# Block-sparse attention with a feed-forward layer: instruction order pinned on every engine, and values gathered from an on-chip copy in place of indirect DMA

## The chip, the cores and the metric

The kernel runs on one core of a Trainium2 chip. Times are device microseconds (us). A kernel's time is the median of its runs; a profile is one execution, with its own span. TensorE does the matrix products, VectorE (DVE) and ScalarE (ACT) the element-wise work, GpSimd (POOL) the gathers, and SyncE (SP) issues transfers. PEclk is the clock that TensorE was granted, as a share of full speed.

## The reference

```python
# q, k, v: [4, 8, 768, 64] float32; blocks of 32, so 24 blocks; 3 random blocks for each query block
mask = |block_i - block_j| <= 1, or block_i or block_j in {0, 23}, or block_j in sampled_blocks[block_i]
attn = softmax(where(mask, q @ k.T / 8, -1e9)) @ v          # per batch and head
x    = attn.transpose(0, 2, 1, 3).reshape(3072, 512)
out  = gelu_exact(x @ w_in[512, 2048]) @ w_out[2048, 512]
```

## The kernel before

A batch is worked in two halves of 384 query rows. For each half, the attention of the next half is merged with the output product of this one, and the hidden layer (x times w_in, 64 matmuls) is merged with "fill" steps: transposes of q and k for the next batch, and gathers. A scheduler decides the final order on each engine from the traced order and its own estimates.

Values are gathered from DRAM, one indirect DMA for each of the 11 query blocks of a half, and keys by two calls on GpSimd for each head pair:

```python
    def gather_v(b, hb, st):
        vg = vg_pool.tile([P, NQH, VROW], BF16, tag="vg", name="vg")
        for i in range(NQH):                       # 11 indirect DMAs
            nc.gpsimd.indirect_dma_start(out=vg[:, i, :], in_=v_dram[b][:, :], in_offset=...idx_v[:, qi:qi + 1]...)

    def gather_k(b, hb, hp, st):
        dv = kg.rearrange("p n (s c) -> p (n s) c", c=BLOCK)
        kv = kt.rearrange("p (n c) -> p n c", c=BLOCK)
        nc.gpsimd.indirect_copy(dv[:, 0:32, :], kv, idx_k[:, hb, 0:2], ...)    # 32 indices of 32 bf16
        nc.gpsimd.indirect_copy(dv[:, 32:44, :], kv, idx_k[:, hb, 2:3], ...)   # 12 indices
```

One q or k tile of a head pair is transposed: VectorE permutes it (`pm`), TensorE transposes six squares into PSUM (`ps`), and VectorE copies the result out (`tk` or `tq`); for k it also copies the two global blocks (`kgl`).

```python
    def transpose_qk(b, hp, which, tile_in, st):
        nc.vector.tensor_copy(pm, tile_in[:, 2 * hp:2 * hp + 2, :].rearrange(...))
        for j in range(NT):
            nc.tensor.transpose(ps[:, j, :], pm[:, j, :, :]..., ident)
        nc.vector.tensor_copy(dst.rearrange(...), ps.rearrange(...))
        if which == "k":
            ...                                    # kgl: two small copies out of dst
# ... cut ...
        merge(hidden_steps(b, hb, st), fill)
        if half + 1 < 2 * B:
            merge(attention_steps(nb_, nhb, sts[nb_]), output_steps(b, hb, st))
```

The softmax here doesn't subtract the row's maximum and nothing guards it: scores larger than these inputs give would overflow.

## Time and profile before

| | before |
|---|---|
| time, median of 3 | 408.56 us (406.87 to 408.6) |
| span of the profiled execution, mean clock | 429.1 us, 0.877 |
| TensorE busy / GpSimd busy | 67% / 48% |
| first hidden layer starts (profile) | 64.3 us |

From the page of the profiled execution: busy time by engine, and the span in 40 slices, where a digit is the busy tenths of a slice (PEclk: tenths of full clock).

```profile
span 429.1 us, 8099 instructions
...
PE 288.6 (67%) x3532; PEld 174.0 (41%) x3568; DVE 148.2 (35%) x327; ACT 142.9 (33%) x192; POOL 206.7 (48%) x212
...
PE   0273279324737376910949967699679999899996
...
POOL 8457675671577745665454373556722055500000
PEclk9999999655686779775899996969979999999999
```

TensorE is full only in the last quarter. The stretches from one hidden layer to the next, by engine (busy us, number of instructions, granted clock, DMA share and GB/s), say how much longer the early stages are than the last undisturbed one, 29.6 us:

```profile
64.00:137.40 73.40, 39.95 (x395) 23.20 (x397) 17.48 (x38) 16.53 (x22) 43.20 (x40) 0.67 0.76 158
137.40:212.90 75.50, 40.14 (x491) 23.63 (x496) 20.91 (x42) 19.34 (x26) 44.15 (x39) 0.75 0.48 107
...
374.70:404.30 29.60, 28.31 (x368) 16.76 (x372) 8.16 (x18) 16.32 (x22) 0.61 (x1) 1.00 0.08 28
```

What engines waited for (total us, times, longest) names two causes: gathered rows that come by indirect DMA, and a VectorE that stands at a value copy until its load has landed, with TensorE behind it for 20.1 us.

```profile
DVE v_pj L235 <- DMA st_v<-in_v_dram: 37.4, 3, 23.0
...
PE og L354 <- DMA vg<-v_dram_186,idx_v: 20.2, 17, 4.7
PE od L376 <- DVE xd L344: 20.1, 1, 20.1
...
PE ps L268 <- DVE pm L264: 7.5, 3, 4.0
```

### The profile page before, as it was taken

The page shows a single profiled execution, that of the slowest core. Times are in us where ns is not written, and L with a number is a line of the kernel's source. Part 1 is how long each engine was busy: PE and PEld are TensorE (multiplying, and loading weights), DVE is VectorE, ACT ScalarE, POOL GpSimd, SP SyncE. Part 2 cuts the span into 40 slices and gives each one's busy share as a digit, 9 for nine tenths or more (in the row PEclk, how much of TensorE's full clock was granted, in tenths as well). Part 3 has the DMA queues.
Part 4 walks back from the last instruction along what each step waited for, and adds up shares of the span by engine and source line. Part 5 has one row for each costly group of instructions (what it writes and reads, how often), then busy time and mean ns, then how long its engine had stood idle before and what let it go on. Part 6 is the DMA issues. An engine that isn't in the chain of part 4 may idle for free. (4 is left out here: it accounts for less than half of the span.)

```text
span 429.1 us, 8099 instructions
## 1 busy us (share of the span) xinstructions
PE 288.6 (67%) x3532; PEld 174.0 (41%) x3568; DVE 148.2 (35%) x327; ACT 142.9 (33%) x192; POOL 206.7 (48%) x212
## 2 busy tenths in 40 slices
PE   0273279324737376910949967699679999899996
PEld 0251165202423143500526534355345556555552
DVE  2693140102713054201514514447224436603301
ACT  1041125502200045510027503643247167267240
POOL 8457675671577745665454373556722055500000
PEclk9999999655686779775899996969979999999999
DMA  8935289139598764225433370501400100000101
GB/s 124 193 82 114 71 134 202 34 104 177 128 187 256 212 80 83 76 62 86 150 112 42 77 226 26 73 26 52 124 14 27 49 2 28 26 26 26 50 2 74
DMA packets 30805, 39.04 MB, mean 91 GB/s; under 512 B 4657, under 2 KB 24369, under 8 KB 30769
## 3 DMA queue, kind: packets, MB, share of 16 engines
q0 software_dynamic: 20960, 25.35, 31.5%
q1 hardware_dynamic: 9616, 13.02, 8.9%
q8 instruction: 28, 0.46, 0.4%
q10 hardware_dynamic: 192, 0.13, 0.1%
q14 instruction: 9, 0.07, 0.0%
HBM read 42.51 MB, written 9.62 MB: 121 GB/s over the span
## 5 line engine op out<-in xcount | busy, mean ns | idle before, releaser
L439 PE MATMUL hp<-xT,w_in_sb 128*128 128x384 bf16 x512 | 94.4, 341 | 27.9 <-ACT g L441 17.5
L286 POOL INDIRECT_COPY kg<-tk,idx_k 128x1024 bf16 x32 | 56.4, 1763 | 112.5 <-issue 44.0
L441 ACT ACTIVATE g<-hp 128x768 bf16<-128x768 f32 x64 | 51.5, 811 | 170.6 <-PE hp L439 76.3
L455 PE MATMUL op<-w_out_sb,g 128*128 128x512 bf16 x348 | 93.2, 396 | 6.0 <-issue 4.2
L439 PEld LDWEIGHTS <-w_in_sb 128*128 128x128 bf16 x512 | 51.5, 102 | 65.5 <-issue 36.0
L455 PEld LDWEIGHTS <-g 128*128 128x128 bf16 x384 | 34.3, 101 | 33.5 <-issue 6.4
L354 PEld LDWEIGHTS <-pt 128*32 128x32 bf16 (+1 forms) x992 | 28.7, 103 | 37.8 <-issue 24.3
L287 POOL INDIRECT_COPY kg<-tk,idx_k 128x384 bf16 x32 | 36.9, 1154 | 14.6 <-issue 13.3
L306 DVE TENSOR_TENSOR pt<-pt,mask_x 128x768 bf16<-128x768 bf16 x32 | 22.9, 723 | 61.0 <-ACT pt L305 58.6
L268 PE MATMUL ps<-ident,pm 128*128 128x128 bf16 x192 | 19.0, 256 | 24.6 <-DVE ident L110 15.9
L269 DVE COPY tk<-ps 128x768 bf16<-128x768 bf16 x16 | 15.3, 955 | 53.8 <-PE ps L268 23.0
L354 PE MATMUL og<-vg,pt 128*32 128x65 bf16 x704 | 18.9, 207 | 20.6 <-DMA vg<-v_dram_186,idx_v 20.2
L459 DVE COPY os<-op 128x512 f32<-128x512 f32 x24 | 16.6, 690 | 33.2 <-PE op L455 26.2
L256 POOL DMA_INDIRECT vg<-v_dram_189,idx_v x22 | 21.2, 963 | 12.9 <-PE og L354 6.7
L256 POOL DMA_INDIRECT vg<-v_dram_188,idx_v x22 | 21.4, 973 | 12.4 <-PE og L354 6.4
L268 PEld LDWEIGHTS <-pm 128*128 128x128 bf16 x192 | 15.3, 115 | 27.6 <-DVE pm L264 14.4
L256 POOL DMA_INDIRECT vg<-v_dram_187,idx_v x22 | 21.8, 989 | 7.4 <-issue 6.4
L376 PE MATMUL od<-v_nat,pd 128*64 128x65 bf16 x192 | 11.1, 215 | 20.1 <-DVE xd L344 20.1
L256 POOL DMA_INDIRECT vg<-v_dram_186,idx_v x22 | 21.3, 968 | 6.5 <-issue 6.5
L343 DVE RECIPROCAL rc<-og 128x6 f32<-128x6 f32 x32 | 6.1, 192 | 46.8 <-PE og L354 46.7
L316 PEld LDWEIGHTS <-kg 64*128 64x128 bf16 x704 | 12.7, 96 | 19.0 <-POOL kg L286 7.3
L376 PEld LDWEIGHTS <-pd 128*64 128x64 bf16 x192 | 9.1, 127 | 23.5 <-issue 22.6
(333 smaller groups left out, 347.4 us busy)
## 6 DMA issues: line engine op xcount, KB each, us to landing
out_dram<-os SPq DMA_DIRECT2D x24, 256.0 KB
st_v<-in_v_dram POOLq DMA_DIRECT2D x4, 768.0 KB
st_k<-in_k_dram POOLq DMA_DIRECT2D x3, 768.0 KB
st_q<-in_q_dram POOLq DMA_DIRECT2D x3, 768.0 KB
w_in_sb<-in_moe_w_in_dram POOLq DMA_DIRECT2D x4, 512.0 KB
w_out_sb<-in_moe_w_out_dram POOLq DMA_DIRECT2D x4, 512.0 KB
v_dram_186<-v_pj SPq DMA_DIRECT2D x1, 780.0 KB
v_nat<-v_dram_186 SPq DMA_DIRECT2D x1, 780.0 KB
```

The lines of the kernel that those rows point to most:

```text
L256: nc.gpsimd.indirect_dma_start(out=vg[:, i, :], out_offset=None, in_=v_dram[b][:, :], in_offset=bass.IndirectOffsetOnAxis(ap=idx_v[:, qi:q ...
L268: nc.tensor.transpose(ps[:, j, :], pm[:, j, :, :].rearrange("p h d -> p (h d)"), ident)
L269: nc.vector.tensor_copy(dst.rearrange("p (n j) -> p n j", j=NT), ps.rearrange("p j n -> p n j"))
L286: nc.gpsimd.indirect_copy(dv[:, 0:32, :], kv, idx_k[:, hb, 0:2], i_know_this_is_slow=True)
L287: nc.gpsimd.indirect_copy(dv[:, 32:44, :], kv, idx_k[:, hb, 2:3], i_know_this_is_slow=True)
L306: nc.vector.tensor_tensor(pt[:, 0, :, 0:HALF], pt[:, 0, :, 0:HALF], mask_x[:, hb * MH:hb * MH + MH, :].rearrange("p m c -> p (m c)") .unsq ...
L354: nc.tensor.matmul(o, lhsT=l, rhs=r, start=first, stop=True, skip_group_check=True)
L376: nc.tensor.matmul(od[:, 0, h, :], lhsT=pd[:, h, t, :], rhs=v_nat[:, t, 2 * hp + h, :], start=(t == 0 and h == 0), stop=True, skip_group_c ...
L439: nc.tensor.matmul(hp_[:, i, 0:HALF], lhsT=w_in_sb[:, ki, (m + i) * P:(m + i + 1) * P], rhs=xT[:, ki, :], start=(ki == 0), stop=(ki == KIN ...
L441: nc.scalar.activation(g[:, m:m + 2, :], hp_[:, :, 0:HALF], AF.Gelu)
L455: nc.tensor.matmul(op, lhsT=g[:, k, ti * P:ti * P + P], rhs=w_out_sb[:, k, :], start=(k == 0), stop=(k == KOUT - 1))
L459: nc.vector.tensor_copy(os, op)
```

## The change

The intent: (1) hold every engine to the traced order, so that nothing waits at a late load that the trace places later; (2) remove the 88 indirect DMAs: the values of a batch are written to DRAM once, spread onto the chip four times, rotated, over four groups of 32 partitions (16 transfers of 192 KB), and gathered from there by GpSimd in three calls for each half; (3) gather keys in one call with pairs of bf16 taken as f32; (4) refine the merging: more and smaller steps. The diff, cut to its core:

```diff
+class InOrder:
+    def __getattr__(self, name):
+        f = getattr(self._eng, name)
+        def call(*args, **kwargs):
+            return self._tc.keep_in_program_order(f(*args, **kwargs))
+        return call
...
+    pe, dve, act, pool, sp = (
+        InOrder(tc, e) for e in (nc.tensor, nc.vector, nc.scalar, nc.gpsimd, nc.sync))
...
+    def spread_v(b):
+        for c in range(4):
+            for s in range(4):
+                i = 6 * ((c - s) % 4)
+                sp.dma_start(out=v_rep[32 * s:32 * s + 32, i:i + 6, :],
+                             in_=v_dram[b][:, :].rearrange("(t c r) w -> c r t w", c=4, r=BLOCK)[c])
+    def natural_v(b, eng):                     # v_nat and vgl: copies of v_rep in natural order
...
     def gather_v(...):
-        for i in range(NQH):
-            nc.gpsimd.indirect_dma_start(...)
+        pool.indirect_copy(v_gat[hb].bitcast(F32)[...], v_rep.bitcast(F32)...,
+                           idx_v[:, hb, 2 * c:2 * c + 2], ...)      # c = 0, 1, 2
...
     def gather_k(...):
-        nc.gpsimd.indirect_copy(dv[:, 0:32, :], kv, idx_k[:, hb, 0:2], ...)
-        nc.gpsimd.indirect_copy(dv[:, 32:44, :], kv, idx_k[:, hb, 2:3], ...)
+        pool.indirect_copy(kg.bitcast(F32)..., st["k", hp].bitcast(F32)..., idx_k[:, hb, 0:3], ...)
...
+            if hb == 0:
+                fill += gv + gk                 # gathers of the next half, values first
+                if more:
+                    fill.append(prep_v(b + 1)); fill.append(spread_v(b + 1))
+                    if b > 0:
+                        fill += transpose_steps(b + 1)[:6]
+            elif b == 0:
+                for hp in range(NPAIR):
+                    fill += tr[2 * hp:2 * hp + 2] + [gk[hp]]
+                fill += gv + [lambda: natural_v(b + 1, dve)]
+            else:
+                fill += ([natural_v(b + 1, dve)] + transpose_steps(b + 1)[6:] if more else []) + gv + gk
```

In the start, in the changed kernel, ScalarE makes the first natural-order copies, and the first batch's eight q and k loads come as f32 by the SyncE and ScalarE queues.

## The prediction

> **What bounds it now.** TensorE, but only where it is fed. Busy times by 10 us stretch: from 340 to 420 us it is 92 to 100% busy at full clock; from 80 to 210 us about half, and the granted clock falls to 0.5 in stalls (mean 0.877). The undisturbed stage (second half of the last batch) takes 29.7 us from hidden layer to hidden layer in the chain of work that ended last. Eight stages of 30 to 34 us need about 250 us; the profile shows 364 us from the first hidden layer (64 us) to the end, so about 110 us are stalls. The timelines name them:
> - Pool: eleven indirect DMAs per half, 1.26 us apart (13.9 us), TensorE following row by row (38–47, 85–97 us); four key gathers, 5.19 us each start to start (20.8 us).
> - Order: VectorE stands at a value copy waiting for its load (37.4 us in the groups, longest 23.0); TensorE idles 20.1 us at 184–204 us.
>
> **What the change does.** It removes the 88 indirect DMAs (111 us of Pool) and adds 24 gathers from a fourfold on-chip copy, refilled by 3.1 MB of DMA per batch. Key gathers become one 44-index call in f32. From the trace, 32 indices take 3.65 us and 12 take 1.52 (start to start, 32 elements each): 0.107 us an index. The Trainium skill (GPSIMD Engine Reference, section Performance pitfalls for Q7 kernels) gives about 102 cycles per small read command, so I take it as mostly per index: estimated 4.5 us per key gather, 10 us per half for values. Pool then needs about 28 us per half plus 2.4 of load issues, against 35 before: still close to TensorE's 31. If the cost is per element, it is 21 us and Pool is off the path.
>
> Pinned order removes the waits at late loads, runs gathers a half ahead, and interleaves finer. One exponential less per head pair (0.27 us) is off the path. At the start, weighted sums still wait for value write, spread and three gathers: first hidden layer at about 55 us against 64.
>
> New costs: VectorE gets the natural-order copies, and its two-input and two-port operations collide with denser gathers (Trainium skill, SBUF — State Buffer, section Who interferes with whom). The trace agrees: the mask product took 2.54 us under a gather, 0.56 alone. Six of a batch's transposes sit in the last three hidden steps; at about 1.75 us of VectorE each (0.4 + 0.95 + 0.4) they hold the in-order TensorE some 6 us per batch.
>
> **Sum.** 55 start + 250 TensorE stages + 10 VectorE-bound transposes + 10 waiting for Pool (mostly values in batch 1) + 4 tail = 329 us in a profile. The profiled run of before was 5% above the timed ones; a kernel with fewer DMA waits should lose less, so I take 2%.
>
> Predicted **322 us, 8 in 10 between 300 and 348**. Faster by over 2%: 0.96; within 2%: 0.025; slower: 0.015.
>
> **What would show it.** Right: TensorE busy above 85% and mean clock near 0.97 after 60 us; key gathers about 4.5 us start to start; longest TensorE waits on gathered values in batch 1 and on VectorE at the ends of even hidden stages; no 20 us hole. Wrong: key gathers at 2.6 us with Pool idle half the time (then about 305); or Pool solid and TensorE waiting on gathered tiles in every half (then about 345).
>
> **What would make it wrong.** Gather cost per call; port collisions stretching VectorE and Pool; the refill of the copy landing late, so that value gathers slip a stage; loads queued behind waiting gathers on Pool.

## The result, and the profile after

| | before | after |
|---|---|---|
| median, same chip | 407.99 us (406.87 to 408.6) | 374.64 us (369.54 to 377.65) |
| ratio of the fast runs | | 0.909, 95% interval 0.902 to 0.916 |
| span of the profile, clock | 429.1 us, 0.877 | 375.9 us, 0.962 |
| TensorE / GpSimd busy | 67% / 48% | 76% / 29% |
| first hidden layer | 64.3 us | 71.7 us |

A ratio is the mean time of one kernel's fast runs over that of the other's in the same rounds, so it is not quite the ratio of the medians. The kernel became 9% faster here (14% on a chip where the kernel before is slower: ratio 0.863 in `a0_control`), and the time lies 27 us above the top of the predicted range of 348.

The profile of after fell into a run counted slow (two of the four were, at 377 us and clock 0.96; the fast ones took 369.5 and 372.3). For comparisons of stages I therefore use the profile of an unaltered copy run later, `a0_control`. From the page of after:

```profile
span 375.9 us, 8258 instructions
...
PE 284.4 (76%) x3632; PEld 161.5 (43%) x3632; DVE 164.7 (44%) x358; ACT 153.3 (41%) x173; POOL 108.4 (29%) x119
...
PE   0340058699966859786896989876997899999995
...
POOL 8331467430012374320244553100342531000000
PEclk9999999599998979969999999999999999999999
```

What engines waited for in after:

```profile
PE sd L52 <- ACT pt L52: 25.8, 4, 21.9
...
DVE tk L52 <- PE ps L52: 23.7, 13, 8.9
...
PE ps L52 <- DVE pm L52: 21.8, 19, 2.9
ACT v_nat_199 L52 <- DMA v_rep<-v_dram_205: 20.0, 1, 20.0
...
DVE v_pj L52 <- DMA st_v<-in_v_dram: 14.5, 2, 9.0
...
PE og L52 <- POOL v_gat_201 L52: 6.2, 3, 2.5
```

The 20 us hole and the waits for gathered rows are gone. In their place TensorE waits 19 times for `pm`, and VectorE 13 times for `ps`: the two engines now wait for each other. ScalarE stands once for 20 us at the start, at a copy (`v_nat`) that waits for the spread values; TensorE's longest single wait, 21.9 us before `sd`, is for an exponential that stands behind this copy. The stretches from hidden layer to hidden layer in `a0_control`, to be held against those of before:

```profile
73.10:105.30 32.20, 30.95 (x381) 17.12 (x381) 9.44 (x19) 16.34 (x18) 4.75 (x4) 0.96 0.92 185
105.30:158.20 52.90, 39.68 (x530) 21.68 (x529) 29.77 (x59) 19.32 (x22) 21.95 (x17) 0.97 0.35 62
158.20:195.90 37.70, 32.30 (x417) 18.40 (x417) 19.29 (x37) 16.34 (x18) 8.32 (x6) 1.00 0.54 127
195.90:236.40 40.50, 34.95 (x493) 19.30 (x492) 20.33 (x41) 19.33 (x22) 16.92 (x15) 1.00 0.45 79
...
315.00:345.60 30.60, 29.41 (x380) 16.54 (x380) 7.85 (x18) 16.34 (x18) 0.00 (x0) 1.00 0.07 27
...
sum 297.30, PE 255.56 PEld 141.69 DVE 124.62 ACT 129.81 POOL 71.02; mean PE 31.95 PEld 17.71 DVE 15.58 ACT 16.23 POOL 8.88
```

The worst stages fell from 73 and 76 us to 32 and 53. But only the first and the seventh come near 30, and the stretch from the first hidden layer to the end is 297.3 us, where 274 (250 + 10 + 10 + 4) was predicted.

How GpSimd spends its time, by start (us) and duration shown, from the timeline of `a0_control`:

```profile
47.24 1.65 POOL L52 INDIRECT_COPY v_gat<-v_rep,idx_v 128x1024 f32 x1 [6.34 <-issue]
50.90 1.65 POOL L52 INDIRECT_COPY v_gat<-v_rep,idx_v 128x1024 f32 x1 [2.01 <-issue]
54.26 1.44 POOL L52 INDIRECT_COPY v_gat<-v_rep,idx_v 128x768 f32 x1 [1.72 <-issue]
```

The bars last 1.65 us, but starts lie 3.66 us apart. Four consecutive key gathers of after start at 73.65, 76.92, 80.19 and 84.13, the first three 3.27 us apart, with bars of 1.19. The Trainium skill (Perfetto Trace Analysis, GPSIMD Engine Instruction) says that such spans are unreliable and to time by the spacing of starts; this trace agrees: the spacing is 2 to 3 times the bar. By the spacing, the four key gathers and three value gathers of a half take about 23 us (4 x 3.27 + 10), where the prediction had 28, or 21 if the cost went by element.

### The profile page after: what moved, and what is told of

The parts are those of the page before. It is cut to its first block, busy times and chain, and to the rows that moved or that the text cites. A ratio compares the mean times of both kernels' runs of the same rounds, so it can differ in the third digit from the quotient of the medians.

```text
span 375.9 us, 8258 instructions
## 1 busy us (share of the span) xinstructions
PE 284.4 (76%) x3632; PEld 161.5 (43%) x3632; DVE 164.7 (44%) x358; ACT 153.3 (41%) x173; POOL 108.4 (29%) x119
## 5 line engine op out<-in xcount | busy, mean ns | idle before, releaser
L52 PE MATMUL op<-w_out_sb,g 128*128 128x512 bf16 x384 | 106.7, 385 | 0.0
L52 PE MATMUL hp<-xT,w_in_sb 128*128 128x384 bf16 x512 | 92.7, 340 | 7.5 <-DVE xT L52 7.5
L52 POOL INDIRECT_COPY kg<-tk,idx_k 128x704 f32 x32 | 40.8, 1276 | 109.4 <-issue 72.6
L52 DVE TENSOR_TENSOR pt<-pt,mask_x 128x768 bf16<-128x768 bf16 x32 | 28.8, 899 | 85.0 <-ACT pt L52 85.0
L52 POOL INDIRECT_COPY v_gat_201<-v_rep,idx_v 128x1024 f32 (+1 forms) x12 | 19.7, 1640 | 69.1 <-issue 35.6
L52 PEld LDWEIGHTS <-pt 128*32 128x32 bf16 (+2 forms) x1024 | 26.2, 100 | 18.5 <-issue 6.8
L52 PEld LDWEIGHTS <-tk 64*128 64x128 bf16 x384 | 10.7, 100 | 46.3 <-issue 45.6
L52 POOL INDIRECT_COPY v_gat_202<-v_rep,idx_v 128x1024 f32 (+1 forms) x12 | 19.6, 1636 | 21.4 <-issue 8.7
L52 PE MATMUL sd<-tq,tk 64*128 64x64 bf16 x192 | 6.2, 202 | 25.8 <-ACT pt L52 25.8
L52 ACT ACTIVATE pd<-sd 128x768 bf16<-128x768 f32 x16 | 13.0, 813 | 19.4 <-PE sd L52 19.4
L52 DVE COPY tq<-ps 128x768 bf16<-128x768 bf16 x16 | 15.3, 958 | 7.4 <-PE ps L52 7.2
L52 DVE TENSOR_TENSOR x<-og,rc 128x384 bf16<-128x384 f32 x32 | 17.8, 557 | 1.1
L52 PEld LDWEIGHTS <-kg 64*128 64x128 bf16 x704 | 11.2, 94 | 12.9 <-issue 10.3
## 6 DMA issues: line engine op xcount, KB each, us to landing
st_v<-in_v_dram POOLq DMA_DIRECT2D x4, 768.0 KB, 15.2
```

The source lines that it names most:

```text
L52: return self._tc.keep_in_program_order(f(*args, **kwargs))
```

## The experiments

All runs are of single kernels on one core; each is timed in three rounds beside the kernel before. The kernel before differs from chip to chip: 407 to 409 us on one, 425 to 433 on two others. The kernel after does not show this: 369.11 us where before took 427.14, and 371.35 where before took 408.47. So I compare times of variants with after directly, mark where a control on the same chip was missing, and give no weight to differences of 2 us.

**Theory A**: the stages are too long because the pinned traced order makes every transpose a serial round trip between VectorE and TensorE. **Rival B**: pins are neutral, the gathers alone set the time. For GpSimd: **off the path**, or **still near the bound**. For the start: **the value copy**, or **the pinned order around it**. (The letters in the expectations are their own: theory A here is theory D there.)

### Controls: the kernel after once more

Two runs of the unaltered kernel, the first beside e5, e7 and c1, the second beside the later start experiments.

> The changed kernel itself, unaltered, as the control on this chip: 367 to 376 us. The kernel before took 408 us on one chip and 428 on another, so the control shows whether the changed kernel moves with the chip too; theory H (the kernel before is longer where DMA lands later, the changed kernel is not) expects it within 1% of 371 us whatever before takes.

> The kernel after, unaltered, as control on the chip of this call: 366 to 376 us, first hidden layer at 70 to 74 us in its profile.

Measured: 369.11 us (367.55 to 372.17), first hidden layer at 73.1; and 371.35 us (368.23 to 373.45), first hidden layer at 71.7. As expected; the base is 369 to 371. Both profiles happen to be of the slowest run of their set. The start varies from execution to execution: in eight profiles with an unedited start (after, both controls, e3, e7, e9, e12, e13) the first value gather starts at 45.7 to 47.2 us and the first hidden layer at 68.8 to 73.1. A start earlier by 4 us in one profile is therefore no evidence by itself.

### e1 and e2: the pins alone, and the gathers alone

```diff
 # e1_unpinned, on after
-            return self._tc.keep_in_program_order(f(*args, **kwargs))
+            return f(*args, **kwargs)
 # e2_before_pinned, on before: the same class around its five engines
```

> The changed kernel with the pins taken out and nothing else changed: the scheduler orders each engine again, the on-chip value gathers stay. Theory A (order and gathers each give part of the gain): 383 to 400 us, a hole of 10 us or more returns on TensorE where VectorE stands at a copy whose load has not landed. Rival B (the gathers give all, pinning gives nothing): within 1.5% of the changed kernel's 371 us. Rival C (pinning costs time, because it forbids overlap): faster than 365 us.

> The kernel before with only the pins added, every engine in its traced order, indirect DMAs kept. Theory A: pinning alone does not help, since the program order of the kernel before puts the value copy first in the fill and the eleven indirect DMAs still take 13.9 us of Pool a half: 400 to 420 us. Rival C (order is the whole gain): 385 us or less.

Measured: without pins 369.22 us, the same as with them, so by time e1's rival B; before with pins 483.38 us, ratio 1.129 (1.122 to 1.136), outside both of e2's ranges. The profile of e1 fell into a run counted slow (376.38 us, the others 367 to 370), so its stages are read with care: its first hidden layer starts at 96.9 us and the rest takes 277 us. So the scheduler's order loses about 24 us at the start (it puts loads and copies of batch 1 first; TensorE waits 41.0 us in four places for gathered values, 31.5 of them once) and gains some 20 in the stages. In e2 VectorE's pinned waits at loads stop TensorE for 128.6 us before `pm` (18 times, longest 42.7). The pins are worth nothing net on the new gathers; they are harmful on the old order, by more than e2's theory A expected. What is shown is that the pins move time from one place to another and add nothing in sum; the gain comes with the rest of the change (on-chip value gathers, the single key call, the finer merging), of which only the key call was run apart (e8).

### e3: the permuting copy one transpose ahead

```diff
         def one(n):
             hp, w = todo[n]
             pm = ahead.pop((b, n), None)
             if pm is None:
                 pm = permute(pair(n), dve)
+            if n + 1 < len(todo) and (b == 1 or n != 5):
+                ahead[b, n + 1] = permute(pair(n + 1), dve)
             transpose_qk(b, hp, w, pair(n), dve, sts[b], pm)
```

> The changed kernel with the permuting copy of the next transpose traced one transpose earlier on VectorE. Theory D (pinned order makes copy, transpose, copy a serial round trip between VectorE and TensorE of about 2.1 us per tile, of which 0.6 us is VectorE waiting for TensorE): the hidden stages with eight or six transposes get 3 to 5 us shorter each, those with two about 1 us; in all 8 to 14 us, 357 to 363 us. Rival E (TensorE waits because VectorE is full, or blocked by gathers, in these stages): under 3 us gained. Rival F (Pool's gathers still bound the stages): no change.

Measured: 361.34 us (359.64 to 363.6), 8 below after, inside the range of the expectation. The waits of TensorE for `pm` (total us, times, longest), in `a0_control` and then in e3:

```profile
PE ps L52 <- DVE pm L52: 22.0, 21, 2.5
```

```profile
PE ps L52 <- DVE pm L52: 9.1, 10, 2.9
```

The time from the first hidden layer on falls from 297.3 to 286.1 us, and the gain lies where it should: the hidden stages with eight and six transposes are 5.1, 3.3 and 3.3 us shorter, those with two are not. Theory A holds. How the round trip looks, in a hidden stage of batch 1, first TensorE and then VectorE in `a0_control` (start, duration, operation; in brackets the idle time before it and what ended it):

```profile
167.06 0.51 PE L52 MATMUL ps<-ident,pm 128*128 128x128 bf16 x6 [0.61 <-DVE pm L52]
168.89 0.51 PE L52 MATMUL ps<-ident,pm 128*128 128x128 bf16 x6 [1.32 <-DVE pm L52]
...
171.29 0.51 PE L52 MATMUL ps<-ident,pm 128*128 128x128 bf16 x6 [0.59 <-DVE pm L52]
```

```profile
168.48 0.35 DVE L52 COPY pm<-st 128x768 bf16<-128x768 bf16 x1
169.50 0.96 DVE L52 COPY tk<-ps 128x768 bf16<-128x768 bf16 x1 [0.67 <-PE ps L52]
170.49 0.36 DVE L52 COPY kgl<-tk 64x64 bf16<-64x64 bf16 x2
170.87 0.36 DVE L52 COPY pm<-st 128x768 bf16<-128x768 bf16 x1
171.84 0.96 DVE L52 COPY tq<-ps 128x768 bf16<-128x768 bf16 x1 [0.60 <-PE ps L52]
```

Follow one k tile: `pm` at 168.48, the six transposes from 168.89, copy out at 169.50, `kgl` at 170.49, and only then the next `pm` at 170.87, which lets TensorE go on at 171.29. A k tile takes 2.4 us and a q tile 1.85, with VectorE waiting 0.6 us in each and TensorE waiting 0.6 or 1.3. All of this is written in the traced order: one `transpose_qk` after the other. The scheduler of before, and of e1, had moved `pm` forward (TensorE waits for it three times in before, twice in e1).

### e7 and e12: the natural-order copies behind the transposes

```diff
-fill += ([natural_v(b + 1, dve)] + transpose_steps(b + 1)[6:] if more else []) + gv + gk
+fill += (transpose_steps(b + 1)[6:] + [natural_v(b + 1, dve)] if more else []) + gv + gk
 # e7_nat_last: this alone.  e12_pm_nl: this and e3's edit
```

> The changed kernel with the natural-order value copies traced after the two transposes of the odd hidden stages of batches 1 and 2, not before. Theory D (TensorE follows VectorE through the pinned order): hidden stages 3 and 5 of 15.2 and 14.8 us go to about 13 us, 3 to 5 us less in all. Rival: the copies only move into the attention stage and delay the weighted sums there, no gain.

> Two edits together on the kernel after: the permuting copy one transpose ahead, and the natural-order value copies behind the two transposes in odd hidden stages. The first alone gave 361.3, the second alone 370.7 (nothing). Theory (the round trips hide the value copies: VectorE is idle inside them anyway, so the copies only show when the round trips are gone): together 352 to 358, more than the sum of the single gains. Rival (the two are independent): 360 to 363.

Measured: e7 370.72 us (no gain in time); e12 351.01 us (349.83 to 354.32; no control on that chip), which is 10 less than e3 alone. e7's expectation missed in time. In its profile the two odd hidden stages that it aims at do fall, to 13.6 and 13.8 us, but three others are 1.2 to 1.4 us longer at a lower granted clock (0.79 to 0.92, against 0.88 to 1.00 in `a0_control`). e12 came out 1 us below its range: the two edits are not independent. Of the 10 us to e3, 7.6 lie in the two odd hidden stages and 3.2 in the start, which neither edit touches. In sum these two stages take 30.0 us in `a0_control`, 30.1 in e3, 27.4 in e7 and 22.5 in e12. VectorE of e12 in a stage with six transposes, as above:

```profile
158.82 0.36 DVE L52 COPY pm<-st 128x768 bf16<-128x768 bf16 x1
159.09 0.95 DVE L52 COPY tq<-ps 128x768 bf16<-128x768 bf16 x1
159.96 0.35 DVE L52 COPY pm<-st 128x768 bf16<-128x768 bf16 x1
160.23 0.95 DVE L52 COPY tk<-ps 128x768 bf16<-128x768 bf16 x1
161.21 0.36 DVE L52 COPY kgl<-tk 64x64 bf16<-64x64 bf16 x2
```

There is no idle time in brackets any more: VectorE works without gaps, `pm` of the next tile stands ahead of the copy out, and a stage's 64 hidden matmuls and six transposes take 13.5 us in place of 16.8. With two transposes (odd halves) they take 11.2, in place of 14.9 to 15.2.

### e4: the closing copy on ScalarE

```diff
-        dve.tensor_copy(st["xT", hb][:, :, c], st["xdT"][...])
+        act.copy(st["xT", hb][:, :, c], st["xdT"][...])
```

> The changed kernel with the small copy that closes each attention stage (xT from xdT, 0.2 us undisturbed, 2.2 and 2.4 us under gathers) done by ScalarE. Theory G ([...]TensorE waits 2 to 3 us and the next ten microseconds run at a lower clock): the waits of hp for xT of 2.6 and 3.1 us go to about 1 us or less, 4 to 8 us in all, 363 to 367 us. Rival: the last x copies bound that point anyway, under 2 us.

Measured: 369.69 us, no gain, as its rival had said. The slow copy that it was built for is real: in after it took 2.21 and 2.44 us under gathers of GpSimd and 0.18 to 0.28 at other times. The Trainium skill (SBUF — State Buffer, Who interferes with whom) says that VectorE in a two-port mode and GpSimd contend for a shared port pair, which whoever issues first holds for the whole instruction; these times agree with that. With the copy on ScalarE TensorE's wait for `xT` fell from 6.1 to 0.6 us. But its hidden stages are 6.6 us longer in sum than those of `a0_control`: the first six run at a granted clock of 0.80 to 0.96, where the control has 0.88 in the first and 1.00 in the other five. Why the clock was lower is open. The slow copy beside a gather is shown; that it costs the kernel time by itself is not.

### e8 and e9: GpSimd doing more, and less

```diff
 # e8_bf16_gather: key gathers in two bf16 calls as in the kernel before
-        pool.indirect_copy(kg.bitcast(F32)..., idx_k[:, hb, 0:3], ...)
+        pool.indirect_copy(dv[:, 0:32, :], kv, idx_k[:, hb, 0:2], ...)
+        pool.indirect_copy(dv[:, 32:44, :], kv, idx_k[:, hb, 2:3], ...)
 # e9_no_v_gathers: wrong result on purpose
-    [lambda c=c: gather_v(b, hb, c) for c in range(len(VCH))]
+    [lambda c=c: gather_v(b, hb, c) for c in range(len(VCH) if b == 0 else 0)]
```

> The kernel after with each key gather turned back into the two bf16 calls of the kernel before (32 and 12 indices of 32 bf16 elements), everything else as it is. Theory (GpSimd has slack in the changed kernel, 29% busy, and the gather's cost goes by elements): a key gather takes about 5.2 us start to start in place of 3.27, some 62 us more of GpSimd in all, and the time stays near the 369 us of the unaltered kernel: 367 to 379, the few us from the gathers of batch 1, where the waits for gathered values grow by up to 8 us. Rival (GpSimd is still close to the bound, as the prediction's 10 us of waiting for it supposed): each half grows by a good part of its 8 us, 390 us or more.

> The value gathers of batch 1 taken away (18 calls with the others of later halves, whichever the loop issues there); the output is wrong on purpose. Theory (GpSimd off the path apart from the late values of batch 1): TensorE's 4.1 us wait for gathered values in batch 1 goes[...]: 358 to 367 us against about 369. Rival (gathers of values hold every half[...]): 350 us or less. Miss of both: no change within 0.6%.

Measured (no control on that chip): e8 382.25 us (381.36 to 384.42), e9 355.15 us (354.88 to 356.14). Both lie between the theory of an unhindered GpSimd and its rival: some 60 us more of gathers (32 x 1.9) cost 11 to 13 us, and 18 value gathers fewer save 14 to 16. So GpSimd is neither the bound (the 60 us would then have cost most of 60) nor free. Two ways are visible. First, order: TensorE's wait for gathered values grew from 6.2 to 12.8 us in e8 and fell to 2.1 in e9. Batch 1's value gathers are traced behind its key gathers, which wait for transposes, while GpSimd (in after) stands idle from 85 to 109 us. Second, the shared port: beside gathers, some of VectorE's copies inside the round trips grow. VectorE of e8, in a hidden stage of batch 1:

```profile
168.04 0.96 DVE L52 COPY tk<-ps 128x768 bf16<-128x768 bf16 x1 [5.63 <-PE ps L52]
169.03 2.82 DVE L52 COPY kgl<-tk 64x64 bf16<-64x64 bf16 x2
171.88 0.53 DVE L52 COPY pm<-st 128x768 bf16<-128x768 bf16 x1
```

The `kgl` copies that took 0.36 us above took 2.82 here, and that hidden stage 20.9 us in place of 16.8. But the granted clock in it was 0.84, against 1.00 in `a0_control`, and in the profile of after the same stage took 19.6 us at 0.85 without the added gathers, so the copies explain at most a part. Nor did all copies grow in e8: the masked product took 842 ns in the mean (855 in `a0_control`), the natural-order copy 1011 (median; 1535). e9 is clearer: there the masked product fell from 855 to 640 ns, the natural-order copy from 1535 to 954, and the odd hidden stages from 14.9 and 15.2 to 12.5, with the clock at 1.00 in both kernels. Against the profile of `a0_control`, e9 is 5.1 us shorter in these two stages, 6.5 in the stretch where batch 1's late values were waited for, and 4.0 in the start, which it does not edit. That these are collisions at the port is the reading that fits the skill's page named under e4; the runs show the longer durations beside gathers, not the port.

### e13: batch 1's value gathers first

```diff
-                fill += gv + [lambda: natural_v(b + 1, dve)]
+                fill = gv + fill + [lambda: natural_v(b + 1, dve)]
 # together with e12's two edits
```

> As the previous kernel, and in the first half of batch 0 the value gathers for batch 1 are issued ahead of its key gathers, without any edit of the start. Theory: the wait for gathered values in batch 1 (4.1 us in the kernel after) goes: 347 to 354, and what is left to the 340.3 us of the combined kernel (7 to 14 us) is what the three edits of the start give together, although the first of them alone gave 0.6 us. Rival (the combined kernel owes its time to the higher granted clock and to the stages, nothing to the start): 339 to 344.

Measured: 347.28 us (345.49 to 347.65), 3.7 below e12 on the same chip, just inside its theory's range: moving the value gathers was worth that much, and it was a matter of order alone. (The stretch that uses these values fell from 33.9 to 27.1 us in the profile; part was lost again in the two hidden stages before it, where the granted clock was 0.81 and 0.91, against 0.88 and 1.00 in e12.)

### e5, e15: the start's loads

```diff
 # e5_w_in_later: w_in loads after the last key gather of the start
-        else:
-            load_w_in(hp - 1)
-    load_w_in(3)
+    for c in range(4):
+        load_w_in(c)
 # e15_v_first: q and k loads of the third and fourth head pair behind the value write
-    for hp in range(NPAIR):
+    for hp in range(2):
         first_st["k", hp] = load_first("k", hp, sp)
...
             prep_v(0, first_v)
+            for i in range(2, NPAIR):
+                first_st["k", i] = load_first("k", i, sp)
+                first_st["q", i] = load_first("q", i, act)
             spread_v(0)
```

> The changed kernel with the four loads of w_in issued after the last key gather of the start instead of between them. Theory S (the fourfold spread of the values is late because these loads share the DMA engines with it): the value gathers start 4 to 7 us earlier than at 44 us, the first hidden stage at 65 to 68 us instead of 72, 3 to 6 us less in all. Rival (the spread is bound by its own issue and its waits for earlier transfers): no change, or a loss if w_in lands too late.

> The kernel after, with the loads of q and k of the third and fourth head pair issued behind the write of the reordered values instead of at the top. Theory (the value load is late because it shares the DMA with eight 384 KB loads): it lands at about 11 us in place of 15, everything behind it moves up by 3 to 4 us, first hidden layer at 67 to 70 us, time 364 to 367. Rival (the same bytes must move before the spread ends, or the late loads now hold the transposes of the last head pairs): no change within 1 us, or slower.

Measured: e5's first hidden layer starts at 66.5 us in place of 73.1, but its time is 368.46, 0.6 below its control and within noise. e15's starts at 67.6 in place of 71.7, time 367.06 with a control of 371.35, some 4 us, though one of its runs (372.69) was counted slow. The time fits its theory, the way does not: the copy that waits for the value load starts at 15.8 us in place of 18.5, but the first value gather only 1.1 us earlier (44.8 against 45.9). With the spread of unedited starts (68.8 to 73.1) and c2 below, its gain is not shown.

### e14 and e16: the start without the value copy's transfers

Both leave out batch 0's sixteen spreading transfers, so batch 0's result is wrong; they differ in what fills the copy instead.

```diff
 # e14_no_spread0
+            dve.memset(v_rep, 0.5)
             prep_v(0, first_v)
-            spread_v(0)
 # e16_no_spread_split
+            dve.memset(v_rep[:, 0:8, :], 0.5)
+            pool.memset(v_rep[:, 8:16, :], 0.5)
             prep_v(0, first_v)
-            spread_v(0)
         if hp == 2:
+            act.copy(v_rep[:, 16:24, :], v_rep[:, 0:8, :])
```

> The kernel after, with batch 0's sixteen spreading transfers replaced by one VectorE memset of the on-chip copy (wrong result on purpose for batch 0; the load, the reordering copy and the write to DRAM stay). Theory (the start is the chain of the value copy): ScalarE's copy and the value gathers no longer wait until 43 to 47 us, the first hidden layer starts at 54 to 60 us in place of 72, and the time falls by 10 us or more, to 352 to 360. Rival (transposes, index arithmetic and the 17 us of attention behind them set the start in any case): first hidden layer at 66 us or later, time 363 or more.

> The kernel after, without batch 0's sixteen spreading transfers; the on-chip copy is filled by a VectorE memset (8 columns), a GpSimd memset (8 columns) and a ScalarE copy (8 columns) at places where these engines stand idle in the trace of the kernel after (wrong result on purpose for batch 0). Theory (the transfers of the value copy set when the weighted sums can start, and GpSimd's last key gather, which ends at about 40.7 us, is the next limit): the first value gather starts at 40 to 42 us in place of 46 to 47, the first hidden layer at 63 to 67 us in place of 72 to 73, the time falls by 4 to 9 us to 361 to 367. So the transfers are worth some 6 of the 17 us, and the rest is the pinned order itself. Rival (the transfers are worth the whole difference): first hidden layer at 58 us or earlier, 357 us or less. Second rival (nothing): 368 to 372.

e14 measured 374.31 us, first hidden layer at 73.5: by the letter its rival, in truth a spoilt experiment. Its stand-in held VectorE for 10.7 us in the pinned order, so the transposes came as much later as the transfers would have let things start earlier:

```profile
15.36 10.72 DVE L52 MEMSET v_rep<- 128x12800 bf16 x1 [2.62 <-POOL kg L52]
26.11 0.96 DVE L52 COPY v_pj<-st_v 128x3072 bf16<-128x3072 bf16 x1
```

e16 fills the same memory where three engines stood idle, and measured 367.05 us (366.03 to 367.73) beside the control's 371.35; its first hidden layer starts at 65.9 us. GpSimd in its start:

```profile
38.28 1.19 POOL L52 INDIRECT_COPY kg<-tk,idx_k 128x704 f32 x1 [5.09 <-DVE pt L52]
...
43.22 1.64 POOL L52 INDIRECT_COPY v_gat<-v_rep,idx_v 128x1024 f32 x1 [1.67 <-issue]
...
49.84 1.43 POOL L52 INDIRECT_COPY v_gat<-v_rep,idx_v 128x768 f32 x1 [1.32 <-issue]
```

Value gathers now start at 43.2 us, right behind the last key gather, which waited for VectorE; from there on nothing is gained. So the transfers are worth 2.5 to 4 us: the first value gather starts at 43.2 in place of 45.7 to 47.2, and the time is 4 us shorter. The other 3 us of the earlier hidden layer are not theirs: the attention behind the gathers takes 14.6 us here and 17.3 in `a0_control`, but 14.5 in e12, whose start is not edited. What remains is order, by the trace and not by a test: a last key gather at 38 us, three value gathers (about 10 us), and the attention behind them, which in the pinned order is done one head pair after another (before needed 9 us from its last gathered tile to the hidden layer, with other pairs' scores and exponentials already done).

### c1 and c2: the edits together

c1_combined has the edits of e3, e4, e5, e7 and e13, and the start's natural-order copies on VectorE instead of ScalarE (`natural_v(0, dve)`), so that exponentials do not queue behind them. c2 adds e15's.

> The changed kernel with five edits together: permuting copies one transpose ahead, closing copy on ScalarE, w_in later, natural-order copies last in the odd hidden stages and on VectorE at the start, value gathers of batch 1 before its key gathers. If theories D, G and S hold and their parts add: first hidden stage at about 65 us, the eight stages in about 270 us, 335 to 345 us. If the parts hide behind one another: 350 us or more.

> The combined kernel (340.3 us) with the same reordering of the first loads. Theory: its first hidden layer moves from 66.8 to 62 to 64 us and its time to 335 to 338. Rival: 339 to 342.

Measured: c1 340.3 us (338.73 to 341.58), 28.8 below its control and 0.796 of before (0.791 to 0.802), correct and inside its expected range. c2 341.28: no further gain, as its rival had said; its first hidden layer starts at 68.1 us, where 62 to 64 was expected. The stages of c1 sum to:

```profile
sum 270.50, PE 251.46 PEld 141.64 DVE 120.74 ACT 131.84 POOL 73.77; mean PE 31.43 PEld 17.71 DVE 15.09 ACT 16.48 POOL 9.22
```

c1 beats both kernels. From e13 to c1 are 7 us, given by the two edits of the start (w_in later, natural-order copies on VectorE) and e4's together, across two chips and without their shares separated. In the profiles c1 is 2.1 us shorter than e13 in the start, 4.4 in the first two hidden stages, where the granted clock is 1.00 in place of 0.81 and 0.91, and 2.7 in the two stretches behind the odd hidden stages of batches 1 and 2, which end with e4's copy and are 0.8 us shorter in e4 too.

## Why the prediction was wrong, point by point

The direction held (faster by more than 2%), and so did the mechanism of the gain in part: indirect DMAs and the 20 us hole were what cost, and both are gone. The prediction also credited the pins with removing waits at late loads; in sum they gain nothing (369.22 us without them, e1). The size was wrong: 322 us was predicted, with 348 as the upper end, and after takes 369 to 375. The steps that failed are terms of the sum. The measured column is worked out from `a0_control`: a hidden stage alone takes 10.6 us (the last two) and each of its 24 transposes 0.33 us of TensorE; the stretches between hidden stages take 20.1 us undisturbed, 24.9 with the dense scores (c1's shortest), and the tail 14.2.

| Term | Predicted | Measured | Off by |
|---|---|---|---|
| start to first hidden layer | 55 | 73.1 | +18 |
| TensorE's own stages and tail | 250 + 4 | 8 x 10.6 + 24 x 0.33 + 4 x 20.1 + 3 x 24.9 + 14.2 = 262 | +8 |
| "VectorE-bound transposes" | 10 | hidden stages are 117.6 in sum, 92.7 of it TensorE's own: 25 | +15 |
| "waiting for Pool" | 10 | stretches between hidden stages, over undisturbed: 11 | +1 |
| profile to timed | minus 2%, 7 us | 370.4 span, 369.1 median: 1 | +6 |

322 + 18 + 8 + 15 + 1 + 6 makes 370. In the second row the stages come to 248 us, as predicted; the tail is 14.2 in place of 4. The 11 us of the fourth row are 7 in batch 1, as predicted, and less than 1 in each of the others. The two terms that carry the miss come first, then two smaller ones and what was right:

1. **"10 VectorE-bound transposes."** The prediction counted VectorE's work (1.75 us for a transpose) and said that it would hold TensorE in the last three hidden steps, "some 6 us per batch". It did not see that the trace writes `pm`, transpose, copy out in series, and that pinning keeps this series: each transpose costs both engines' time plus two hand-overs, 1.85 to 2.4 us. In addition the natural-order copies, which it named as a new cost without giving them a term, stand in front of the transposes in odd halves. e3 (8 us) and e12 (18 to 20, without a control on its chip) show it. Before's profile held the warning, TensorE waiting for `pm` three times only, which the pins would undo.

2. **"55 start."** Measured 72 to 73 in after and its controls. The prediction let the weighted sums wait for value write, spread and three gathers, and left no room for what follows: in `a0_control` the third value gather ends at 55.7 us, when the hidden layer should have started, and 17 us of attention come behind it (14.5 in e12). The 3.1 MB of spreading transfers were named and got no time of their own: from 25 to 43 us the DMA engines of `a0_control` are 90% busy or more in 39 of 40 slices, at a mean of 227 GB/s, with these and the w_in loads, and value gathers start at 46 to 47 us. e16 shows the transfers to be worth only 2.5 to 4 of the 18 us; how much each of the other parts is worth was not separated.

3. **GpSimd's cost per gather.** The Trainium skill (GPSIMD Engine Reference, Performance pitfalls for Q7 kernels) gives about 102 cycles for a small read command, and I took the cost to go mostly by index: 4.5 us for a key gather. It is 3.27. Values, 32 indices of 32 elements, take 3.65 in f32, as keys did in bf16 before, and 44 indices of 16 elements take less; two bf16 calls of 44 x 32 elements took 5.16 us in e8. At 32 elements, 32 indices took 3.65 us and 12 took 1.52, so 0.107 for each index more. At 16 elements, 44 indices took 3.27, where a cost by index would give 4.7 (44 x 0.107) and one by element half of that. So the cost is neither, and nearer to the elements; taking it by index was wrong here. GpSimd's busy share of 29% (by the bars, which are too short) agrees with the alternative that the prediction had named, "per element, Pool off the path", but e8 and e9 correct that too: the time does react, by a fifth of the added gathering.

4. **Profile to timed run.** The prediction took the 5% by which the profiled run of before exceeded the timed ones for a cost of profiling. On two other chips before takes 427 to 431 us in the median, as long as that profiled run (430.93), and the profiled run of after is one of its four timed ones. So the chip is the likelier cause; on which chip that profile was taken is not on record.

5. **Right**: the longest waits for gathered values are in batch 1, as the prediction said, and e13 shows that ordering alone removes 3.7 us there; no 20 us hole; the mean clock is 0.96 to 0.98. TensorE "above 85%" busy after 60 us about holds (85% from 60 to 350 us in after; 255.6 of 297.3 us, 86%, in `a0_control`), and so could not tell the good case from the bad. That the 10 us for GpSimd came out at 11 is in part luck, as its gathers took 23 us a half and not 28.

Open: what of the start belongs to which link of the pinned order; why the granted clock was lower in some executions, as in the hidden stages of e4, whose gain it took; and the pins' worth on an order traced with `pm` ahead, for which no unpinned counterpart was run.

## What to carry to other kernels

When an order is pinned, whatever the scheduler had moved forward is written by hand or lost: look in the old profile for the pairs of engines that hardly wait for each other, and check that the new trace still places the first one's work a step ahead. Two edits of one chain can show little apart and more together (the two odd hidden stages: e3 alone nothing, e7 alone 2.6 us, both 7.5); test such edits together. Compare stages, and their granted clock, before a profile's earlier start or longer stage is put down to an edit. An experiment's stand-in must cost nothing in the order that it joins (e14).

## What the Trainium skill lacked or had wrong

- GPSIMD Engine Reference, Performance pitfalls for Q7 kernels: it gives a cost for a small read command, and no page gives the time of an on-chip gather. Here, start to start: 3.27 us for 44 indices of 16 f32, 3.65 us for 32 indices of 32 elements in f32 and in bf16 alike, 5.16 us for 44 indices of 32 bf16 in two calls. The cost goes neither by index alone nor by element alone (point 3).
- DMA: Bandwidth & Descriptors, Specifications, names 512 B as the smallest transfer for line rate and about 358 GB/s as what one core gets of HBM. Packets of 962 B in the mean (4.09 MB in 4252 packets, from 25 to 43 us of `a0_control`) moved at 227 GB/s with the engines 90% busy or more in 39 of 40 slices, so being busy did not mean that rate here. Two kinds of transfer ran at once, so this is no test of either figure.
- SBUF — State Buffer, Who interferes with whom: the rule of the shared ports agrees with what was seen (a copy at 0.18 us took 2.44 beside a gather), and it has no number for what such collisions cost a kernel. Here 18 gathers fewer (e9) shortened the two odd hidden stages by 5.1 us in sum; the rest of its 14 to 16 us lies elsewhere.
- Perfetto Trace Analysis, GPSIMD Engine Instruction: agrees; bars of 1.19 and 1.65 us stood for 3.27 and 3.65.
